# A chunked scan and a gated pair of matrix products on one core: a new order for the first scan, seven-product blocks for the second group, and an earlier place for each later group's y

## The chip, the core and the metric

The kernel runs on one NeuronCore of a Trainium2 chip. Five engines work side by side, each with its own instruction queue: TensorE (PE, matrix products into the accumulation memory PSUM), VectorE (DVE), ScalarE (ACT), GpSimd (POOL) and SyncE (SP), which here only issues transfers. Instructions on one queue start in the order in which they stand there; between queues, semaphores say when data is ready or a buffer is free.

The metric is the time of one execution on the device in microseconds (us). A profile records one further execution, instruction by instruction.

## The reference, cut to what matters

Two blocks follow each other. The first is a state-space scan over 4 x 8 heads, 768 positions, head size 32 and state size 16, in chunks. The second takes its output as 3072 tokens of 256 features and applies two matrix products with a gate between them. All is float32.

```python
# x, B, C: (4, 8, 768, 32|16|16);  a: (4, 8, 768), chunks of 32
la  = log(clip(a, 1e-6, 1));  cum = cumsum(la, within the chunk)
L   = exp(cum[i] - cum[j]) where i >= j, else 0
y   = ((C @ B.T) * L) @ x  +  (C @ state) * exp(cum)        # inside + carried in
state = exp(sum(la)) * state + (B * exp(cum[-1] - cum)).T @ x

x  = y as (3072, 256)
h  = x @ w_in                      # (3072, 2048)
g  = h * sigmoid(1.702 * h)
out = g @ w_out                    # (3072, 256)
```

## The kernel before, in words

**Tokens and groups.** The kernel works in chunks of 64 positions (two in a tile of 128), takes 256 positions as a *pair* (of tiles) and 512 tokens as a *group*: 12 pairs, 6 groups, two pairs to a group. Group 0 is pairs 0 and 1, group 1 is pairs 2 and 3, and so on. While the matrix products of group g run, the scan of the pairs of group g+1 and the loads of group g+2 are put between them. The order on each engine is the order in which the Python code issues the instructions (`in_order` ties each to the one before on its engine).

**One pair of the scan.** `differ` and `exps` (pairs 0 and 1) or `decay` (later pairs, a VectorE scan of 2.28 us) make the tile `L` of decay factors; `turn_only` transposes B and C on TensorE (`tp`, L514) and ScalarE or VectorE copies them out (L519, L521); `gain` (L591) multiplies B and x into the increments `A`, `keep` (L610, L622) adds them up to the states `S`; `score` (L560) multiplies C and B; `weigh` (L571) multiplies the scores into `L` on VectorE; `since_start` (L546) scales C; `finish` then makes y: `inter(0)` and `inter(1)` (L649) for what the states carry in, `intra` (L678) for what lies inside a chunk, in small matrix products on parts of the array, and two ScalarE copies (L702) to `yT`. A tiny GpSimd `memset` of `spare` (L666) stands between `inter(0)` and `inter(1)` as an order mark. Pair 1 is finished with `late=True`: `intra` first, then both `inter`.

**The weights** come as 64-bit numbers and are turned to float32 piece by piece, ten pieces in all: `fields` (L161, L164), `rounded` (L177) and `join` (L188, L194) on VectorE, `clamp` (L172, L173) on ScalarE. `narrow(i)` is rounded(i), fields(i+1), join(i).

**First product, plainly.** `hidden(g, f)` (L723) makes 128 hidden features for all 512 tokens with two products of 128 x 512; ScalarE applies the gate. `half` (L737) does it for 256 tokens of group 0, so that work can begin when only pair 0 is ready. Group 0 and group 1 use this form.

**First product, by seven.** For groups 2 to 5, `first(g, j, i)` treats a block of 256 features x 512 tokens as a 2 x 2 matrix of parts and uses seven products of 128 x 256 in place of eight. The steps `j.1 j.6 j.7 j.4` (L795) add up in one PSUM bank, `X`, and ScalarE copies the running sum out after each of the first three (L800: `ac`, `b`, `ac`), so each of them waits for the copy of the one before. The steps `j.5 j.2 j.3` (L805) add up in a second bank, `Y`. Then `j.D` (VectorE) adds `ac` to `Y`, a second addition (VectorE, inside `j.3`) adds `b`, and `j.S`, `j.T` and the end of `j.4` are ScalarE's gate. The sums of parts that this needs are `mix_in` of the weights (L757) and `mix_y` of `yT` (L763 to L765), on VectorE.

**Second product.** Group 0: `project_all` (L837). Groups 1 to 5: `product` (L896), again by seven, on sums `mix_w` of `w_out` (L862) and `mix_g` of the hidden block. A step `P` in the strings below is one of the seven products of one block: two of 128 x 128, four instructions in the records, since each float32 product is recorded as two.

**PSUM.** Products that don't add up over a whole group share four banks (`bank`, pool `ps`); a new tile waits until the readers of the tile that held its bank before are done.

**The order around the change.** The very first scan is written out call by call. Group 1 ran through a list of `H` (two `hidden`) and `P` (seven products of a block) with other work after each in `after`: the scan's `finish(later)` after `H3`. For later groups a string names the steps; the part that matters reads (block 2 and 3 of the first product, with `y` the scan of the next group and `w` its `weigh`):

```python
"2.1 1.S 1.4 1.3 2.6 2.5 2.2 2.7 1.T s 2.D 2.S w 2.4 3.1 2.3 3.5 2.T M0 3.6 "
"refill 3.7 y 3.2 3.D along 4.1 P P 3.4 P 3.S 4.6 P 3.3 4.5 3.T M1 P P 4.7 P 4.2 4.D M2"
```

Of the kernel before, what the change touches and what calls it, by code (L numbers as in the profile page):

```python
# [35 lines left out]
def kernel(  # L36
# [130 lines left out]
    def clamp(i):  # L167


        e = power[i]  # L170
        z = e.bitcast(FP32)
        nc.scalar.activation(z, e, AF.Relu, scale=-8.0, bias=edge[:, 0:1])  # L172
        nc.scalar.activation(e, z, AF.Relu, scale=-1.0, bias=edge[:, 1:2])  # L173
# [366 lines left out]
    def since_start(p, engine=nc.vector):  # L540

        b, c = divmod(2 * p, NC)
        s = st[p]
        tp = s.pop("tp")
        s["CsT"] = ssd.tile([P, 2, P], FP32, tag="CsT", name=f"CsT{p}", bufs=3)
        engine.tensor_tensor(out=s["CsT"], in0=tp, in1=since[b][:, c:c + 2], op=ALU.mult)  # L546
# [19 lines left out]
    def weigh(p, ks=(slice(0, 2),)):  # L566

        Lv = Ls[p].rearrange("p k r q i -> p k r (q i)")
        cb = st[p]["cb"].rearrange("p r k e -> p k r e")
        for k in ks:  # L570
            nc.vector.tensor_tensor(out=Lv[:, k], in0=Lv[:, k], in1=cb[:, k], op=ALU.mult)  # L571
# [51 lines left out]
                    out=new[:, m], in0=old, scalar=since[b][:, c + k, e:e + 1],  # L623
                    in1=new[:, m], op0=ALU.mult, op1=ALU.add)

    def finish(pairs, late=False):


        g, first = divmod(pairs[0], PG)
        y = [bank(f"y{pairs[0]}_{i}")[:, :NK * len(pairs) * 2 * H].rearrange(  # L630
            "p (t k i) -> p t k i", t=NK, i=H) for i in range(2)]
        begun, halves, seen = set(), {}, []

        def begin(i, parts):
            new = not begun & {(i, q) for q in parts}
            begun.update((i, q) for q in parts)
            return new

        def inter(flip):

            for n, p in enumerate(pairs):
                for k in range(2):
                    for i in range(2):
                        m, t = 2 * k + i, i ^ flip
                        if (4 * p + m) % (2 * NC) == 0:
                            continue
                        old = state[p][:, m - 1] if m else state[p - 1][:, 3]
                        rows = slice(HB * N * t, HB * N * (t + 1))
                        nc.tensor.matmul(  # L649
                            out=y[i][:, t, 2 * n + k], lhsT=old[rows],  # L650
                            rhs=st[p]["CsT"][rows, k, SIDES[i]],
                            start=begin(i, range(HB)), stop=False,
                            tile_position=(HB * N * t, 0), skip_group_check=True)
                        ins = tc.nc.cur_bb.bb.instructions[-1]
                        if not flip:
                            halves[i] = ins
                        elif seen:
                            tie(ins, seen.pop())

        def tie(ins, other):  # L660
            tc.add_manual_dep(ins, other.name, mybir.DependencyInfo(
                mybir.DependencyClass.Sync, mybir.DependencyReason.DATA), reason="same_bank")

        def part():

            nc.gpsimd.memset(spare, 0.0)  # L666
            ins = tc.nc.cur_bb.bb.instructions[-1]
            for other in halves.values():
                tie(ins, other)
            seen.append(ins)  # L670

        def intra(n, p):
            L = Ls[p]
            for k in range(2):
                for h in range(NH):
                    t, q = divmod(h, HB)
                    for i, side in enumerate(SIDES):
                        nc.tensor.matmul(  # L678
                            out=y[i][D * q:D * q + D, t, 2 * n + k], lhsT=rx[p][side, k, h],
                            rhs=L[side, k, h // Q, h % Q],  # L680
                            start=begin(i, (q,)), stop=True, tile_position=(H * i, D * q),
                            skip_group_check=True)

        if first == 0:
            yT[g] = ffn.tile([P, NK, TG], FP32, tag="yT", name=f"yT{g}")
        if not late:
            inter(0)
            part()
        for n, p in enumerate(pairs):
            intra(n, p)  # L690
        if late:
            inter(0)
            part()
        inter(1)
        for p in pairs:
            state.pop(p - 1, None)
            st.pop(p)
            Ls.pop(p)
        cols = slice(2 * first * P, 2 * (first + len(pairs)) * P)
        to = early_y if pairs[0] == 0 else yT[g][:, :, cols]  # L700
        for i in range(2):
            nc.scalar.activation(  # L702
                to.rearrange("p t (k s i) -> p s t k i", s=2, i=H)[:, i], y[i], AF.Copy)
        if pairs[0] == 0:
            nc.gpsimd.tensor_copy(yT[g][:, :, cols], to)
# [295 lines left out]
    ends(0, 0, nc.gpsimd)  # L1001
    ends(0, 1, nc.gpsimd)
    weigh(0)
    turn_only(1, ("ACT", "ACT", "ACT"))
    gain((0,))
    for r in range(2, R):
        ab[1, r] = bank(f"ab1_{r}")[:, :2 * Q * H]
# [1 line left out]
    differ(1, [(r, ab[1, r]) for r in range(2, R)])  # L1009
    exps(1, range(2, R))  # L1010
    since_start(0, nc.gpsimd)
    since_start(1, nc.gpsimd)
    keep(0)
    join(0)
    fields(1)
    score((1,))
    ends(1, 0)
    ends(1, 1)
    weigh(1, (0,))
    finish((0,))  # L1020
    clamp(1)
    table(AF.Silu)
    gain((1,))
    keep(1, (0, 1, 2))
    half(0, 0)
    weigh(1, (1,))
    finish((1,), late=True)
    rounded(1)
    join(1)
    load(PG)  # L1030
    spread_rows(1)
    fields(2)
    clamp(2)
    half(1, 0)
    keep(1, (3,))


# [31 lines left out]
       lambda: weigh(PG), lambda: weigh(PG + 1))  # L1069
    at(in_project[0], 9, lambda: narrow(9))  # L1070
    at(in_project[0], 11, lambda: finish(pairs))
    for i in range(4):
        at(in_project[0], 14, lambda i=i: mix_in(i))
    for k in range(PG):
        at(in_project[0], 8 + k, lambda k=k: load(2 * PG + k))
    for k, i in enumerate((9, 13)):
# [6 lines left out]
    at(after, "H0", lambda: decay(n), lambda: decay(n + 1), lambda: turn(n), lambda: turn(n + 1))  # L1083
    at(after, "H1", lambda: gain(later), lambda: score(later), lambda: keep(n),
       lambda: keep(n + 1), lambda: weigh(n), lambda: weigh(n + 1), lambda: spread(3 * PG))
    at(after, "H3", lambda: finish(later), lambda: load(p + 1), lambda: spread(3 * PG + 1))
    for k, i in enumerate(("H4", "P0", "P2", "P4")):
        at(after, i, lambda k=k: mix_w(k))
    for j in range(NF // 2):
        if j < 7:  # L1090
            at(after, f"P{min(j - 1, 4)}" if j else "H4", lambda j=j: mix_g(1, j))
    for k in range(PG):
        at(after, f"P{2 * k}", lambda k=k: decay(3 * PG + k))
    at(after, "P3", lambda: clip_rows(2), lambda: decay_rows(2))
    assert [b for b in range(NB) if 3 * CG <= b * NC < 4 * CG] == [2]


# [7 lines left out]
    project_all(0, in_project[0])  # L1105
    load(p)
    spread_rows(2)
    for step in "H0 H1 H2 H3 H4 P0 H5 P1 H6 P2 H7 P3 P4".split():
        j = int(step[1:])
        if step[0] == "H":  # L1110
            hidden(1, 2 * j)
            hidden(1, 2 * j + 1)
        else:
            product(1, j)
        for do in after.get(step, []):
            do()

    def run(g, steps, products=(), **do):
# [13 lines left out]
    def seven(g, j):  # L1132
        return [(g, j, (i,)) for i in ORDER]

    def ahead(g, p=None):

        pairs = (p, p + 1) if p else ()
        for k in pairs:
            turn_only(k)
        if pairs:  # L1140
            gain(pairs)
        for k in pairs:
            since_start(k)
        mix_y(g)
        for k in pairs:
            keep(k)

    run(1, "P P A P P P P P", seven(1, 5), A=lambda: ahead(2, p))
    mix_g(1, 7)

    for g in range(2, NG):
# [20 lines left out]

        if more:

            run(g, "2.1 1.S 1.4 1.3 2.6 2.5 2.2 2.7 1.T s 2.D 2.S w 2.4 3.1 2.3 3.5 2.T M0 3.6 "
                "refill 3.7 y 3.2 3.D along 4.1 P P 3.4 P 3.S 4.6 P 3.3 4.5 3.T M1 P P 4.7 P 4.2 4.D M2",
                seven(g, 0), s=lambda: score((n, n + 1)), w=lambda: (weigh(n), weigh(n + 1)),
                y=lambda: finish((n, n + 1)), refill=refill, along=along,
                M0=lambda: mix_g(g, 0), M1=lambda: mix_g(g, 1), M2=lambda: mix_g(g, 2))
            if most:  # L1180
                decay(p)
        else:
            run(g, "2.1 1.S 1.4 1.3 2.6 2.5 2.2 2.7 1.T 2.D M0 3.1 3.5 2.S 2.4 3.6 2.3 3.2 3.7 2.T 3.D M1",
                M0=lambda: mix_g(g, 0), M1=lambda: mix_g(g, 1))
        for j in range(5 if more else 4, NF // 2):
            h = "{1}.1 {0}.S P {0}.4 P {1}.6 P {0}.3 P {1}.7 {0}.T P {1}.5 P {1}.2 P {1}.D M".format(j - 1, j)
            run(g, h, seven(g, j - 4), M=lambda: mix_g(g, j - 2))
            if most and j == 6:
                decay(p + 1)
        k = NF // 2 - 1  # L1190
        run(g, f"P {k}.S P {k}.4 P P {k}.3 {k}.T P P P", seven(g, 4))
        if not more:
            for j in range(k - 1, k + 1):
                mix_g(g, j)
# [38 lines left out]
```

## Time and profile before

| | |
|---|---|
| time, median of 11 runs | 380.1 us (377.56 to 381.24) |
| profiled execution: its time, its span | 381.86 us, 380.1 us |
| TensorE busy | 369.0 us (97%), 3698 products |
| VectorE / ScalarE / GpSimd busy | 244.0 (64%) / 144.1 (38%) / 11.9 us (3%) |
| mean granted TensorE clock | 0.972 of full speed |
| transferred | 25.03 MB, mean 66 GB/s |

The span runs from the first to the last instruction; all times below are from its start. TensorE is busy nearly all the time, so the question in each stage is what the products there cost, how long it stands still, and at which clock it runs. The page draws the granted clock in 40 slices; a table of stretches gives it for any window. The end of a product in the records is modelled, so the distance from one start to the next is the better measure.

The stages, as the timeline of TensorE shows them: first scan to 31 us; group 0's first product to 56 us and second to 91 us; group 1 from 91 to 146 us (its blocks 2 to 7, with second products between, from 101 us); groups 2 to 5 from there, the scan of the next group at about 165, 226 and 284 us in groups 2, 3 and 4.

### The profile page before, as it was taken

The page shows a single profiled execution, that of the slowest core. Times are in us where ns is not written, and L with a number is a line of the kernel's source. Part 1 is how long each engine was busy: PE and PEld are TensorE (multiplying, and loading weights), DVE is VectorE, ACT ScalarE, POOL GpSimd, SP SyncE. Part 2 cuts the span into 40 slices and gives each one's busy share as a digit, 9 for nine tenths or more (in the row PEclk, how much of TensorE's full clock was granted, in tenths as well). Part 3 has the DMA queues.
Part 4 walks back from the last instruction along what each step waited for, and adds up shares of the span by engine and source line. Part 5 has one row for each costly group of instructions (what it writes and reads, how often), then busy time and mean ns, then how long its engine had stood idle before and what let it go on. Part 6 is the DMA issues. An engine that isn't in the chain of part 4 may idle for free.

```text
span 380.1 us, 8605 instructions
## 1 busy us (share of the span) xinstructions
PE 369.0 (97%) x3698; PEld 307.8 (81%) x3698; DVE 244.0 (64%) x457; ACT 144.1 (38%) x317; POOL 11.9 (3%) x42
## 2 busy tenths in 40 slices
PE   8799999999999999989999989999989999999996
PEld 4577448787567789879999969999968999989995
DVE  5877996996898617546776483766582436184453
ACT  5448836210432113533433353433353432363320
POOL 5210000000000000000000000000000000000000
PEclk9759999999999999988999999999999999999999
DMA  8888499025847100057100043000010000010001
GB/s 150 218 278 195 155 183 185 8 60 146 157 76 136 38 5 2 0 103 123 55 2 3 0 85 85 2 2 0 2 57 2 3 0 2 0 58 0 2 0 57
DMA packets 86029, 25.03 MB, mean 66 GB/s; under 512 B 76136, under 2 KB 79464, under 8 KB 85992
## 3 DMA queue, kind: packets, MB, share of 16 engines
q1 hardware_dynamic: 83544, 24.09, 28.6%
q10 hardware_dynamic: 2448, 0.39, 0.6%
q8 instruction: 29, 0.48, 0.5%
q14 instruction: 8, 0.07, 0.1%
HBM read 21.23 MB, written 3.24 MB: 64 GB/s over the span
## 4 chain that ended last, share of the span: by engine, by line
PE 82%; DVE 8%; DMA 4%; SPq 3%; ACT 1%; issue 1%; POOL 0%; DVEq 0%; POOLq 0%
PE acc L896 33%; PE X L795 13%; PE Y L805 10%; PE h L723 7%; PE o L837 5%; PE y L649 4%; PE y L678 3%; PE h L737 2%; DVE L L571 2%; PE cb L560 2%; SPq L123 1%; DMA b<-in_B_dram 1%; PE A L591 1%; DMA c<-in_C_dram 1%; PE tp L514 1%
## 5 line engine op out<-in xcount | busy, mean ns | idle before, releaser
L896 PEld LDWEIGHTS acc<-mw,mg 128*128 128x128 f32 x480 | 65.9, 191 | 3.5
L896 PE MATMUL acc<-mw,mg 128*128 128x128 f32 x480 | 67.6, 275 | 0.0
L914 DVE TENSOR_TENSOR gT<-Y,ac 128x512 f32<-128x512 f32 x32 | 22.1, 691 | 52.5 <-PE Y L805 50.6
L800 ACT ACTIVATE ac<-X 128x256 f32<-128x256 f32 x64 | 24.5, 383 | 74.9 <-PE X L795 74.4
L723 PE MATMUL h<-yT,w_in 128*128 128x512 f32 x112 | 49.9, 595 | 0.0
L896 PEld LDWEIGHTS acc<-w_out,gT 128*128 128x128 f32 x320 | 44.6, 195 | 4.2 <-issue 1.9
L896 PE MATMUL acc<-w_out,gT 128*128 128x128 f32 x320 | 45.5, 278 | 0.0
L772 ACT ACTIVATE gT<-gT 128x512 f32<-128x512 f32 x64 | 33.3, 520 | 27.3 <-DVE gT L914 26.9
L795 PE MATMUL X<-my,mi 128*128 128x256 f32 x128 | 38.6, 383 | 3.4 <-ACT b L800 3.4
L723 PEld LDWEIGHTS h<-yT,w_in 128*128 128x128 f32 x112 | 20.6, 190 | 23.0 <-issue 21.2
L914 DVE TENSOR_TENSOR gT<-Y,b 128x256 f32<-128x256 f32 x32 | 13.5, 422 | 31.1 <-PE Y L805 31.1
L726 ACT ACTIVATE gT<-h 128x512 f32<-128x512 f32 x28 | 16.6, 596 | 44.1 <-PE h L723 44.0
L763 DVE TENSOR_TENSOR mg<-gT 128x512 f32<-128x512 f32 x40 | 27.3, 683 | 8.7 <-PE acc L896 8.7
L837 PE MATMUL o<-w_out,gT 128*128 128x256 f32 x128 | 28.8, 381 | 0.0
L837 PEld LDWEIGHTS o<-w_out,gT 128*128 128x128 f32 x128 | 23.9, 190 | 3.4 <-issue 0.2
L795 PEld LDWEIGHTS X<-my,mi 128*128 128x128 f32 x128 | 20.1, 191 | 5.8 <-ACT b L800 4.6
L896 PE MATMUL acc<-mw,gT 128*128 128x128 f32 x160 | 24.3, 277 | 0.0
L896 PE MATMUL acc<-w_out,mg 128*128 128x128 f32 x160 | 24.0, 275 | 0.0
L896 PEld LDWEIGHTS acc<-mw,gT 128*128 128x128 f32 x160 | 22.7, 191 | 1.5
L896 PEld LDWEIGHTS acc<-w_out,mg 128*128 128x128 f32 x160 | 22.8, 191 | 1.2
L356 DVE TENSOR_TENSOR_SCAN L<-a,idents 128x1024 f32<-128x1024 f32 x9 | 20.5, 2283 | 0.0
L805 PE MATMUL Y<-yT,w_in 128*128 128x256 f32 x64 | 19.9, 394 | 0.0
(137 smaller groups left out, 521.8 us busy)
## 6 DMA issues: line engine op xcount, KB each, us to landing
a<-scratch SPq DMA_DIRECT2D x18, 256.0 KB
bits<-in_moe_w_out_dram SPq DMA_DIRECT2D x4, 1024.0 KB
x<-in_x_dram SPq DMA_DIRECT2D x24, 128.0 KB
out_dram<-c SPq DMA_DIRECT2D x9, 256.0 KB
bits<-in_moe_w_in_dram SPq DMA_DIRECT2D x4, 512.0 KB
bits<-in_moe_w_in_dram SPq DMA_DIRECT2D x2, 1024.0 KB
b<-in_B_dram SPq DMA_DIRECT2D x24, 64.0 KB
c<-in_C_dram SPq DMA_DIRECT2D x22, 64.0 KB
```

The costliest lines, as they stand in the source:

```text
L356: nc.vector.tensor_tensor_scan(out=L, data0=ra[p].rearrange("p k e -> p (k e)"), data1=idents.rearrange("p h i -> p (h i)"), initial=0.0, ...
L649: nc.tensor.matmul(out=y[i][:, t, 2 * n + k], lhsT=old[rows], rhs=st[p]["CsT"][rows, k, SIDES[i]], start=begin(i, range(HB)), stop=False, ...
L723: nc.tensor.matmul(out=h, lhsT=w_in[:, k, f * P:(f + 1) * P], rhs=yT[g][:, k], start=(k == 0), stop=(k == NK - 1))
L726: nc.scalar.activation(gT[g, j][:, i], h, AF.Silu, scale=GELU_SCALE)
L763: nc.vector.tensor_tensor(out=t[:, 0:2], in0=B[:, :, 1], in1=B[:, 0], op=ALU.subtract)
L772: nc.scalar.activation(o, i, AF.Silu, scale=GELU_SCALE)
L795: nc.tensor.matmul(out=s["X"], lhsT=lhsT, rhs=rhs, start=i == "1", stop=i == "4", skip_group_check=True)
L800: nc.scalar.activation(copy, s["X"], AF.Copy)
L805: nc.tensor.matmul(out=o, lhsT=lhsT, rhs=rhs, start=s.pop("new", False), stop=i != "5", skip_group_check=True)
L837: nc.tensor.matmul(out=o[k // 2][:, k % 2], lhsT=gT[g, f // 2][:, f % 2, k * P:(k + 1) * P], rhs=w_out[:, f], start=(f == 0 and k % 2 == 0 ...
L896: nc.tensor.matmul(out=acc[g][0][i][:, cols], lhsT=h[:, cols], rhs=w, start=(j == 0 and i in (0, 2, 5, 6) and k == 0), stop=(j == NF // 2 ...
L914: nc.vector.tensor_tensor(out=o, in0=v, in1=w, op=ALU.add)
```

## The change

**First scan.** Pair 1's transposes (`turn_only(1)`) move from before `gain((0,))` to behind the differences and exponentials of both pairs. Pair 1's `since_start` moves back; `ends(1, ...)` moves before `join(0)`, `gain((1,))` before `score((1,))`, `keep(1, ...)` is cut in other places, `weigh(1)` is done at once, and pair 1 is finished behind `half(1, 0)` in the ordinary order (`inter(0)`, `intra`, `inter(1)`): the argument `late` goes.

**Group 1.** Blocks 0 and 1 stay as they are; blocks 2 to 7 use the seven products. Blocks 2 and 3 run interleaved before the scan's y, block 4 with the second product of block 0, blocks 5 to 7 in the same pattern as later groups (now named `steady` and `closing`). `mix_y(1)` is new, `mix_in(0)` moves to the end of the group, and the loads and VectorE work that hung on `after` are spread anew.

**Later groups.** In block 3 the step `3.2` and `y` now stand between `3.6` and `3.7`; the loads (`refill`) follow y.

```diff
-    def finish(pairs, late=False):
+    def finish(pairs):
...
-        if not late:
-            inter(0)
-            part()
+        inter(0)
+
+        nc.gpsimd.memset(spare, 0.0)
+        seen.append(tc.nc.cur_bb.bb.instructions[-1])
+        for other in halves.values():
+            tie(seen[0], other)
         for n, p in enumerate(pairs):
             intra(n, p)
-        if late:
-            inter(0)
-            part()
         inter(1)
@@ first scan
     weigh(0)
-    turn_only(1, ("ACT", "ACT", "ACT"))
     gain((0,))
     for r in range(2, R):
         ab[1, r] = bank(f"ab1_{r}")[:, :2 * Q * H]
...
     exps(1, range(2, R))
     since_start(0, nc.gpsimd)
-    since_start(1, nc.gpsimd)
+    turn_only(1, ("ACT", "ACT", "ACT"))
     keep(0)
-    join(0)
-    fields(1)
-    score((1,))
     ends(1, 0)
     ends(1, 1)
-    weigh(1, (0,))
+    join(0)
     finish((0,))
+    fields(1)
+    gain((1,))
+    score((1,))
+    since_start(1, nc.gpsimd)
     clamp(1)
     table(AF.Silu)
-    gain((1,))
-    keep(1, (0, 1, 2))
     half(0, 0)
-    weigh(1, (1,))
-    finish((1,), late=True)
     rounded(1)
+    keep(1, (0,))
     join(1)
+    keep(1, (1, 2))
+    half(1, 0)
+    weigh(1)
     load(PG)
     spread_rows(1)
     fields(2)
+    finish((1,))
     clamp(2)
-    half(1, 0)
     keep(1, (3,))
@@ sums for group 1
-    for i in range(4):
-        at(in_project[0], 14, lambda i=i: mix_in(i))
+    at(in_project[0], 14, lambda: mix_in(1), lambda: mix_y(1), lambda: mix_in(2),
+       lambda: mix_in(3))
@@ group 1
-    for step in "H0 H1 H2 H3 H4 P0 H5 P1 H6 P2 H7 P3 P4".split():
...
+    for step in "H0", "H1":
+        for i in range(2):
+            hidden(1, 2 * int(step[1:]) + i)
+        for do in after[step]:
+            do()
...
+    def steady(j):
+        return "{1}.1 {0}.S P {0}.4 P {1}.6 P {0}.3 P {1}.7 {0}.T P {1}.5 P {1}.2 P {1}.D M".format(
+            j - 1, j)
+
+    def closing(k):
+        return f"P {k}.S P {k}.4 P P {k}.3 {k}.T P P P"
...
+    run(1, "2.1 3.1 2.5 2.6 3.6 2.2 2.7 3.5 3.7 3.2 2.D 2.4 3.D 3.4 2.S 3.S y L 2.3 2.T 3.3 3.T",
+        y=lambda: finish(later), L=more_loads)
+    mix_w(0)
+    for j in range(2):
+        mix_g(1, j)
+    run(1, "4.1 P P 4.6 P P 4.7 P 4.5 P 4.2 P 4.D", seven(1, 0))
+    mix_w(1)
+    mix_g(1, 2)
+    decay(p)
+    between = {5: (lambda: mix_g(1, 3), lambda: mix_w(2), lambda: clip_rows(2),
+                   lambda: decay_rows(2)),
+               6: (lambda: mix_g(1, 4), lambda: decay(p + 1)),
+               7: (lambda: mix_g(1, 5), lambda: mix_w(3))}
+    for j in range(5, NF // 2):
+        run(1, steady(j), seven(1, j - 4), M=lambda: [do() for do in between[j]])
+    k = NF // 2 - 1
+    run(1, closing(k), seven(1, 4))
+    mix_g(1, 6)
+    mix_in(0)
@@ later groups
-            run(g, "2.1 1.S 1.4 1.3 2.6 2.5 2.2 2.7 1.T s 2.D 2.S w 2.4 3.1 2.3 3.5 2.T M0 3.6 "
-                "refill 3.7 y 3.2 3.D along 4.1 P P 3.4 P 3.S 4.6 P 3.3 4.5 3.T M1 P P 4.7 P 4.2 4.D M2",
+            run(g, "2.1 1.S 1.4 1.3 2.6 2.5 2.2 2.7 1.T s 2.D 2.S w 2.4 3.1 2.3 3.5 2.T M0 3.6 3.2 y "
+                "refill 3.7 3.D along 4.1 P P 3.4 P 3.S 4.6 P 3.3 4.5 3.T M1 P P 4.7 P 4.2 4.D M2",
```

More of the change, by code (lines that the diff above doesn't have):

```diff
@@ L662, in tie @@
                 mybir.DependencyClass.Sync, mybir.DependencyReason.DATA), reason="same_bank")
[L664 to L670, printed above, removed]
         def intra(n, p):
@@ L1085 @@
        lambda: keep(n + 1), lambda: weigh(n), lambda: weigh(n + 1), lambda: spread(3 * PG))
[L1086 to L1094, printed above, removed]
     assert [b for b in range(NB) if 3 * CG <= b * NC < 4 * CG] == [2]
@@ L1107 @@
     spread_rows(2)
-    for step in "H0 H1 H2 H3 H4 P0 H5 P1 H6 P2 H7 P3 P4".split():
[L1109 to L1115, printed above, removed]
+    for step in "H0", "H1":
+        for i in range(2):
+            hidden(1, 2 * int(step[1:]) + i)
+        for do in after[step]:
             do()
@@ L1146, in ahead, with more_loads @@
             keep(k)
+    def more_loads():
+        load(p + 1)
+        spread(p + 1)
+    run(1, "2.1 3.1 2.5 2.6 3.6 2.2 2.7 3.5 3.7 3.2 2.D 2.4 3.D 3.4 2.S 3.S y L 2.3 2.T 3.3 3.T",
[17 more added lines that the diff above has]
+    mix_in(0)
     run(1, "P P A P P P P P", seven(1, 5), A=lambda: ahead(2, p))
@@ L1185 @@
         for j in range(5 if more else 4, NF // 2):
-            h = "{1}.1 {0}.S P {0}.4 P {1}.6 P {0}.3 P {1}.7 {0}.T P {1}.5 P {1}.2 P {1}.D M".format(j - 1, j)
-            run(g, h, seven(g, j - 4), M=lambda: mix_g(g, j - 2))
+            run(g, steady(j), seven(g, j - 4), M=lambda: mix_g(g, j - 2))
             if most and j == 6:
@@ L1190 @@
         k = NF // 2 - 1
-        run(g, f"P {k}.S P {k}.4 P P {k}.3 {k}.T P P P", seven(g, 4))
+        run(g, closing(k), seven(g, 4))
         if not more:
```

## The prediction

> **What bounds the kernel now.** I read the page's engine shares and clock row first, then the waits of TensorE alone, then the timeline at those waits, then tables of stretches for their clock.
>
> ```profile
> PE 369.0 (97%) x3698; PEld 307.8 (81%) x3698; DVE 244.0 (64%) x457; ACT 144.1 (38%) x317; POOL 11.9 (3%) x42
> ...
> PEclk9759999999999999988999999999999999999999
> ```
>
> TensorE is the bound, so a microsecond counts if it leaves TensorE's work, a standstill or half speed. The clock row has two dips, in slices of 9.5 us.
>
> ```profile
> PE X L795 <- ACT b L800: 3.4, 3, 1.1
> PE tp L514 <- DMA c<-in_C_dram: 1.5, 1, 1.5
> ```
>
> The waits (us in all, times, longest): block 3's X waits for ScalarE's copy `b` once in each of groups 2, 3, 4, and pair 1's transposes wait for C's transfer.
>
> ```profile
> 186.31 0.60 PE L795 MATMUL X<-my,w_in 128*128 128x256 f32 x2
> 186.74 0.61 PE L896 MATMUL acc<-w_out,gT 128*128 128x128 f32 x4
> 187.19 0.60 PE L795 MATMUL X<-my,mi 128*128 128x256 f32 x2
> ...
> 224.37 0.59 PE L795 MATMUL X<-my,mi 128*128 128x256 f32 x2
> ...
> 225.69 0.37 ACT L800 ACTIVATE b<-X 128x256 f32<-128x256 f32 x1
> 226.11 0.70 PE L795 MATMUL X<-my,mi 128*128 128x256 f32 x2 [1.15 <-ACT b L800]
> 226.74 1.11 PE L649 MATMUL y<-CsT,S 64*128 64x64 f32 x14
> ...
> 230.78 0.70 PE L795 MATMUL X<-yT,w_in 128*128 128x256 f32 x2
> ```
>
> In the timeline (start, length), a step of the seven takes 0.43 (186.31 to 186.74), a P 0.45 (186.74 to 187.19). At 224.37 step 3.6 starts; 3.7 must wait until 226.11, because ScalarE's queue held 2.T for VectorE's addition; y follows at 226.74, block 4's first product at 230.78.
>
> ```profile
> 14.00:15.00 1.00, 0.79 (x34) 0.31 (x18) 0.52 (x2) 1.00 (x4) 0.00 (x0) 0.50 1.14 197
> 27.00:28.00 1.00, 1.00 (x27) 0.73 (x10) 0.96 (x5) 0.00 (x0) 0.00 (x0) 0.70 1.00 80
> 164.15:167.56 3.41, 2.27 (x55) 1.64 (x54) 2.05 (x5) 1.07 (x3) 0.24 (x2) 1.00 0.55 55
> 167.56:174.38 6.82, 6.82 (x134) 6.17 (x122) 1.57 (x3) 1.47 (x3) 0.85 (x3) 0.50 0.68 131
> ```
>
> Columns: us, then busy time of TensorE, its loads, VectorE, ScalarE, GpSimd, then granted clock. It is 0.50 from about 14 to 27.6 and from 167.56 to 174.38: 4 and 2 steps of 3.41. Before each drop a window of that length held a standstill and small products: 1.55 idle before the first, 1.15 before the second (2.27 busy of 3.41). The stalls of groups 3 and 4 brought no drop.
>
> [...]products overlap in it (186.31 with length 0.60, the next at 186.74), so I price from start to start.
>
> **The change, part by part.**
>
> *y in groups 2 to 4.* No instruction is added; 3.2 and y go ahead of 3.7. Now: 3.6 at 224.37, stall, y, 4.1 at 230.78, so 6.41. After: 3.2 at 224.80. y's first matmul takes the bank of block 2's X, read last by 2.4's end on ScalarE at 223.65, so no wait; the second bank was block 2's Y, freed by the addition that ends at 225.33, so y starts at 225.4 and waits 0.15. y's length is 3.5 (226.74 to 230.23). 3.7 at 228.9 finds `b` (226.06) long done; 4.1 follows at 229.45, before held to 230.78 by y's eviction, which is earlier too. Gain 1.33, three times: −4.0. What is late next: 3.4 waits for the copy of 3.7, done at about 230.3 when P P reach it at 230.77; 3.3 waits for 3.D, ready 231.0, needed 232.5. Both hidden, by 0.5 and 1.5; without the two P the first would cost up to 0.4. `refill`'s DMAs (x and the next loads on SP) keep their order and wait for y's last read of x anyway; nothing of TensorE's is behind them.
>
> *Clock in group 2.* The 1.15 standstill in the window before 167.56 shrinks to about 0.15. If the drop goes with it: 3.6 to 4.1 takes 8.17 there (163.79 to 171.96) against 6.41 in group 3, so 1.76, and the 2.42 from 171.96 to 174.38 hold products of 1.21 at full clock: −3.0; bounds 0 (the drop stays) and −3.4 (half of 6.82).
>
> *First scan.* Pair 1's transposes move behind both pairs' differences, so C's wait of 1.54 is covered by 24 of those products. Step by step at full clock, with this trace's half-clock durations halved: the first differences end at 11.46; gain(0) 0.47; the masks wait for the exponentials, 12.6; differences 0.60 and 0.65, to 13.85; four transposes of 0.22, to 14.7 (c landed at 13.5); y of pair 0 waits for the third state addition on VectorE, 14.9; 0.72 inside and 0.45 carried, 16.25; gain(1) waits for ScalarE's copies of C, 17.05; scores, 17.75; half(0,0) 1.85, to 19.6; half(1,0) waits for join(1) on VectorE (its queue: Be 0.5, join(0) 1.37, fields 0.8, rounded 0.7, keep 0.6, join 1.4), to 20.65, ends 22.55; then keep and weigh (2 × 1.17) on VectorE, and y of pair 1 ends at 24.5, which ends at 28.9 before. Clamp(2) on ScalarE ends at 26.65 for 31.04. From 31.07 VectorE's chain of weight pieces sets group 0's pace almost without a gap, so what it gains stays: A (L591) starts at about 63.8.
>
> ```profile
> 68.33 0.78 PE L591 MATMUL A<-x,Be 64*32 64x64 f32 x54 [0.34 <-DVE CsT L546]
> ```
>
> So −4.4. Bounds: if the clock still halves at 14 until 27.6, half(1,0), now ahead of y of pair 1, costs 3.7 there, and A lands between −2 and +1.9.
>
> *Group 1.* A plain block before:
>
> ```profile
> 118.36 3.60 PE L723 MATMUL h<-yT,w_in 128*128 128x512 f32 x8
> 121.80 1.05 PE L896 MATMUL acc<-w_out,gT 128*128 128x128 f32 x8
> ```
>
> Blocks 2 to 7 lose this (3.44 a block) and get seven products, 7 × 0.43 = 3.01: 0.43 each, −2.6. Added on VectorE: six D and additions (0.69 + 0.42) and `mix_y` (1.5), 8.2; on ScalarE three copies (0.38) a block and gates in more pieces, some 1.4, so 8.4. VectorE is busy most of the time there:
>
> ```profile
> 101.00:111.70 10.70, 10.70 (x191) 6.22 (x176) 10.32 (x25) 2.39 (x4) 0.77 (x2) 1.00 0.48 81
> 124.90:131.40 6.50, 6.50 (x38) 4.59 (x37) 5.18 (x9) 1.20 (x2) 0.32 (x2) 1.00 0.04 8
> ```
>
> VectorE has 0.38 of room in the first stretch (columns as above) and 1.3 of 6.5 in the second, so not all hides. Walking its queue against TensorE's, the standstills are: 2.5 for gain's bank, freed by keep's first addition (102.57), 0.6; y for ScalarE's gates of 2.4 and 3.4, which read its banks, 0.55; block 4 0.6, where `mix_w(0)` and `mix_g` stand on VectorE behind 3.3's addition and P waits for them; 7.6 behind `clip_rows` and the scan of `decay_rows`, 0.15. Together 1.9, so −0.7; bounds −2.6 (all hide) and +2.5 (below). `mix_in(0)` (1.45), last in the group, is done 0.6 before its product; uncovered it would cost up to 1.45.
>
> *Sum*, against the profiled execution's own 381.86: −4.4 −0.7 −4.0 −3.0 = 369.8 (span 368.0). To the median, 380.1, that is −2.7%. The other executions of before run from 377.56[...].
>
> **Rivals.** *Half clock stays in the first scan (or in group 2).* For it: [...]small products still stand at 12 to 18 with waits of 0.65 and 0.3; against it: the wait of 1.54 is gone. The first scan then gives −2 to +1.9: 372.2 to 376.1, about 373.8; if only group 2's stays, 372.8. *Group 1 costs instead of saving.* VectorE's additions come late by what stands ahead of them (mix_g 1.5, decay 2.28, since-scan 1.76), ScalarE's copies are in order behind gates that wait for them, and X waits about 1 in five of the six blocks: −2.6 + 5.1 = +2.5 there, 373.0. For it: three such stalls in the later groups now; against it: groups 2 to 5 run the same pattern in blocks 5 to 7 without a wait in the list. *y's move gains nothing*, its second bank or 4.1 taking the stall over: 373.8. *Slower:* [...]the clock halves there and up to 34/2 = 17 are lost: 387. [...]the largest standstill of my walk there is 0.6, in block 4.
>
> **How the numbers follow.** As sketched, 369.8 (its own range 367.5 to 371.5): 0.55. Half clock in the first scan or group 2: 0.27. Group 1 costs: 0.11. y gains nothing: 0.03. Slower: 0.04. The range, 366.5 to 376, holds the sketch, group 1 with all its standstills hidden (367.9) and a little below, and the next three cases; it leaves out the last and the tails. About 0.3% (1.1 us) is what this kernel's measurement can tell from none. All cases but the last are below 379: faster 0.93, same 0.02 (rivals together), slower 0.05.
>
> **What would show it.** Right: clock 1.00 from 10 to 28 and 164 to 175; the transposes of pair 1 without C's wait; y of pair 1 done near 24.5 and A near 63.8; no `X <- ACT b` in block 3's row of waits; 4.1 starting 5.1 after 3.6; in group 1 blocks 5 to 7 of 7 × 0.435 + 7 × 0.445 = 6.2 where a hidden and a P block take 6.56. Wrong: a dip in the clock's row, A later than 66, a new wait of TensorE for ScalarE's copies or VectorE's additions in 100 to 146, or y waiting for its second bank by more than 0.5.

## The result, and the profile after

| | before | after |
|---|---|---|
| median | 379.21 us (47 runs, 373.5 to 381.62) | 371.74 us (12 runs, 369.86 to 373.68) |
| profiled execution: time, span | 381.86, 380.1 us | 373.68, 371.9 us |
| mean granted clock in it | 0.972 | 0.986 |

The ratio is 0.984 (0.9815 to 0.9862); the medians stand at 0.980. The ratio leaves out runs over 1.5% above the fastest of their kernel, which for before are most of those that lost the clock (ran at half of it) in more than one stretch. The forecast was 369.8, its range 366.5 to 376: 2.7% below the 380.1 measured then, where the medians fell by 2.0%.

The page of the changed kernel, engine shares and clock row:

```profile
PE 363.8 (98%) x3734; PEld 312.4 (84%) x3734; DVE 251.1 (68%) x472; ACT 150.8 (41%) x341; POOL 11.7 (3%) x42
...
PEclk9769999999999999999999999999999999999999
```

The dip of group 2 (slices 18 and 19) is gone; that of the first scan is still there. What TensorE waited for (us in all, times, longest; `issue` marks a standstill for which the records show no wait):

```profile
PE h L729 <- ACT yT L694: 0.7, 1, 0.7
PE y L649 <- issue: 0.5, 1, 0.5
PE Y L797 <- DVE S L610: 0.5, 1, 0.5
...
PE X L787 <- ACT ac L792: 0.2, 1, 0.2
```

The three stalls of block 3 and the wait for C have left the list. Among the new waits are these four of 0.2 to 0.7, three of them in group 1. The timeline of TensorE at block 3 of group 3 (start, length):

```profile
218.85 0.59 PE L787 MATMUL X<-my,mi 128*128 128x256 f32 x2
219.28 0.59 PE L797 MATMUL Y<-yT,w_in 128*128 128x256 f32 x2
219.81 1.16 PE L649 MATMUL y<-CsT,S 64*128 64x64 f32 x14
...
223.35 0.70 PE L787 MATMUL X<-my,mi 128*128 128x256 f32 x2
223.90 0.70 PE L787 MATMUL X<-yT,w_in 128*128 128x256 f32 x2
```

These are 3.6, 3.2, y, 3.7 and 4.1. From 3.6 to 4.1 it is 5.05, where it was 6.41; 3.7 finds its copy done.

The first scan, in a table of stretches (us, busy time of TensorE, its loads, VectorE, ScalarE, GpSimd, then granted clock), and where it ends to tell, at L591 of group 1's scan:

```profile
10.00:13.00 3.00, 2.70 (x98) 1.97 (x96) 2.97 (x5) 2.31 (x5) 1.20 (x2) 1.00 0.94 122
...
14.00:15.00 1.00, 1.00 (x8) 0.65 (x6) 0.93 (x4) 0.66 (x2) 0.00 (x0) 0.62 0.90 330
...
22.00:24.00 2.00, 2.00 (x6) 1.55 (x6) 1.97 (x5) 0.38 (x1) 0.00 (x0) 0.50 1.03 422
24.00:26.00 2.00, 2.00 (x12) 1.48 (x12) 1.96 (x7) 0.37 (x2) 0.00 (x0) 0.88 1.06 425
```
```profile
66.66 0.78 PE L591 MATMUL A<-x,Be 64*32 64x64 f32 x54 [0.34 <-DVE CsT L546]
```

Half clock from 14.24 to 24.48, 10.24 where before had 13.65 (13.96 to 27.61), though TensorE no longer stands still for C. And group 1, from its first plain product to group 2's first step, before and after:

```profile
91.42 3.60 PE L723 MATMUL h<-yT,w_in 128*128 128x512 f32 x8
...
108.21 1.11 PE L649 MATMUL y<-CsT,S 64*128 64x64 f32 x16
...
111.70 3.70 PE L723 MATMUL h<-yT,w_in 128*128 128x512 f32 x8
...
146.16 0.60 PE L795 MATMUL X<-yT,w_in 128*128 128x256 f32 x2
```

```profile
89.76 3.60 PE L715 MATMUL h<-yT,w_in 128*128 128x512 f32 x8
...
101.11 0.67 PE L797 MATMUL Y<-my,mi 128*128 128x256 f32 x2 [0.50 <-DVE S L610]
...
105.71 1.53 PE L649 MATMUL y<-CsT,S 64*128 64x64 f32 x16
107.17 1.48 PE L670 MATMUL y<-L,x 64*32 64x64 f32 x128
108.58 0.66 PE L649 MATMUL y<-CsT,S 64*128 64x64 f32 x7
109.78 0.67 PE L649 MATMUL y<-CsT,S 64*128 64x64 f32 x9 [0.54 <-issue]
110.38 1.13 PE L797 MATMUL Y<-yT,mi 128*128 128x256 f32 x4
...
145.11 0.60 PE L787 MATMUL X<-yT,w_in 128*128 128x256 f32 x2
```

y takes 4.67 here (105.71 to 110.38), where it took 3.49 (108.21 to 111.70) before.

So the span's 8.2 came from three places. Read from start to start in the two traces: up to group 1's first product −1.66 (91.42 to 89.76); group 1 up to group 2's first product +0.61 (54.74 to 55.35); groups 2 to 5, −7.15 (233.94 to 226.79), of which 3 × 1.36 is y's place and the rest, 3.07, the clock of group 2.

### The profile page after: what moved, and what is told of

Read it like the earlier page. It is cut to its first block, busy times and chain, and to the rows that moved or that the text cites. A ratio compares the mean times of both kernels' runs of the same rounds, so it can differ in the third digit from the quotient of the medians.

```text
span 371.9 us, 8716 instructions
## 1 busy us (share of the span) xinstructions
PE 363.8 (98%) x3734; PEld 312.4 (84%) x3734; DVE 251.1 (68%) x472; ACT 150.8 (41%) x341; POOL 11.7 (3%) x42
## 4 chain that ended last, share of the span: by engine, by line
PE 79%; DVE 8%; issue 7%; DMA 2%; ACT 1%; SPq 1%; POOL 0%; DVEq 0%; POOLq 0%
PE acc L888 31%; PE X L787 16%; PE Y L797 12%; PE o L829 5%; PE y L649 4%; PE y L670 2%; PE h L715 2%; PE h L729 2%; PE cb L560 2%; DMA b<-in_B_dram 1%; PE tp L514 1%; PE A L591 1%; DVE m L177 1%; PE busy L386 1%; DVE p L188 1%
## 5 line engine op out<-in xcount | busy, mean ns | idle before, releaser
L792 ACT ACTIVATE ac<-X 128x256 f32<-128x256 f32 x76 | 29.1, 382 | 81.1 <-PE X L787 80.6
L906 DVE TENSOR_TENSOR gT<-Y,ac 128x512 f32<-128x512 f32 x38 | 26.1, 690 | 48.8 <-PE Y L797 36.0
L764 ACT ACTIVATE gT<-gT 128x512 f32<-128x512 f32 (+1 forms) x76 | 39.4, 520 | 36.5 <-DVE gT L906 35.8
L787 PE MATMUL X<-my,mi 128*128 128x256 f32 x152 | 45.7, 383 | 0.2 <-ACT ac L792 0.2
L715 PE MATMUL h<-yT,w_in 128*128 128x512 f32 x64 | 28.5, 595 | 0.2 <-DVE w_in L194 0.2
L787 PEld LDWEIGHTS X<-my,mi 128*128 128x128 f32 x152 | 24.2, 191 | 1.7 <-ACT ac L792 0.3
L715 PEld LDWEIGHTS h<-yT,w_in 128*128 128x128 f32 x64 | 11.8, 190 | 14.1 <-issue 12.2
L797 PE MATMUL Y<-my,mi 128*128 128x256 f32 x76 | 22.8, 382 | 0.6 <-DVE S L610 0.5
L787 PE MATMUL X<-yT,w_in 128*128 128x256 f32 x76 | 22.9, 385 | 0.1
L787 PE MATMUL X<-my,w_in 128*128 128x256 f32 x76 | 22.8, 384 | 0.0
```

The source lines that it names most:

```text
L715: nc.tensor.matmul(out=h, lhsT=w_in[:, k, f * P:(f + 1) * P], rhs=yT[g][:, k], start=(k == 0), stop=(k == NK - 1))
L764: nc.scalar.activation(o, i, AF.Silu, scale=GELU_SCALE)
L787: nc.tensor.matmul(out=s["X"], lhsT=lhsT, rhs=rhs, start=i == "1", stop=i == "4", skip_group_check=True)
L792: nc.scalar.activation(copy, s["X"], AF.Copy)
L797: nc.tensor.matmul(out=o, lhsT=lhsT, rhs=rhs, start=s.pop("new", False), stop=i != "5", skip_group_check=True)
L906: nc.vector.tensor_tensor(out=o, in0=v, in1=w, op=ALU.add)
```

## The experiments

Every run reports its mean granted clock, so its time can be read beside it. In before's profile the clock is at half for 13.65 in the first scan and for 6.83 in group 2, and the mean is 0.972; in those of `y_only` and `y_filled`, with about 13.6 in the first scan and none in group 2, it is 0.980 and 0.982. No profile shows more than that in the first scan, so a mean of 0.977 or less is read here as a loss somewhere else as well. In the table, "full" means a mean of 0.997 or more; the runs of before are those made beside the experiments. Runs of one kernel at full clock still differ by up to 1.9 (`scan_y_filled`; the changed kernel by 1.4), so a single run is good to about 1.

| kernel | first scan | group 1 | y | runs | at full clock: runs, median us | the others: median us | all: median us |
|---|---|---|---|---|---|---|---|
| before | old | plain | old | 63 | 3, 374.0 | 379.7 | 379.5 |
| `scan_only` | new | plain | old | 22 | 9, 374.3 | 377.9 | 376.6 |
| `y_only` | old | plain | new | 6 | 1, 369.2 | 374.1 | 373.5 |
| `scan_y` | new | plain | new | 6 | 1, 370.0 | 373.5 | 373.3 |
| changed kernel (both sets) | new | seven | new | 18 | 11, 370.4 | 372.6 | 370.8 |
| `y_filled` | old | plain | old, stall filled | 21 | 2, 373.5 | 377.7 | 377.5 |
| `y_c_filled` | old, C's wait filled | plain | new | 6 | 3, 370.5 | 372.6 | 371.4 |
| `scan_y_filled` | new, two products more | plain | new | 6 | 6, 371.3 | none | 371.3 |
| `seven_reordered` | new | seven, new order | new | 6 | 4, 368.4 | 371.4 | 368.5 |
| `seven_fill1` | new, one product more | seven, new order | new | 6 | 6, 369.2 | none | 369.2 |
| `seven_fill2` | new, two products more | seven, new order | new | 6 | 6, 370.2 | none | 370.2 |

**One part at a time.** `y_only` is the kernel before with this edit:

```diff
-... M0 3.6 refill 3.7 y 3.2 3.D along ...
+... M0 3.6 3.2 y refill 3.7 3.D along ...
```

> Only the new place of y and 3.2 in groups 2, 3 and 4; first scan and group 1 as before. Theory (the forecast's): 3.7 no longer stalls, 3 x 1.35 = 4.0 us less where the clock of group 2 is full, and the half clock behind the stall of group 2 goes too, so 4.0 or 7.0 less: about 373.6 in all runs, apart from half clock in the first scan, ratio about 0.985. From 3.6 to 4.1 the trace shows 5.06. Rival (the half clock of group 2 comes from y's small products and not from the standstill): 4.0 less, with the dip of the clock still there in a part of the runs, ratio about 0.989.

Median 373.54, ratio 0.982 (0.977 to 0.987). Group 3 shows the gain at its place, 3.6 to 4.1 in 5.05:

```profile
219.32 0.60 PE L795 MATMUL X<-my,mi 128*128 128x256 f32 x2
...
224.37 0.70 PE L795 MATMUL X<-yT,w_in 128*128 128x256 f32 x2
```

Its stretch from 160 to 175 has a clock of 1.00, and no run's mean is below 0.98 (before: 35 of 63 at 0.977 or less). That goes with the theory. At full clock there is only one run, 369.2. The ratio is the whole change's (0.984) within the noise: most of what the change brings comes from this one edit.

`scan_only` is the other half: the functions and calls of the first scan as changed, all else as before.

> Only the first scan in its new order; groups 1 to 5 as before. If the standstill of 1.54 for C brings the half clock of the first scan: a clock of 1.00 from 10 to 28 in most runs and A (L591) near 63.8, 4.4 less. Rival, which the changed kernel's own profile speaks for: half clock comes all the same, since the products of 11 to 14 use only small parts of the array; then A near 66.7, 1.7 less, and as many runs with half clock as before. The dip of group 2 stays in either case in a part of the runs.

Neither prediction fits whole. 9 of 22 runs are at full clock (before 3 of 63), so the new order does make half clock rarer; but those 9 have a median of 374.3, and the three of before 374.0. At equal clock the new order gains nothing. In its profiled execution the first scan had some 3.2 at half clock (0.91 over 10 to 28; L591 at 65.43), and not at 14: the clock held there and fell near 21, behind a standstill that the new order itself makes, where half(1,0) waits for join(1) on VectorE.

```profile
PE h L729 <- DVE w_in L194: 2.2, 1, 2.2
```

So the new order has more than one place at which the clock fell, 14.24 in the changed kernel's profile and near 21 in this one. The profile has a second finding: group 2 was free of half clock (1.00 from 163 to 175) and group 4 had it (0.75 from 284 to 291), behind the same stall:

```profile
278.60 0.70 PE L787 MATMUL X<-my,mi 128*128 128x256 f32 x2 [1.14 <-ACT b L792]
279.23 1.11 PE L649 MATMUL y<-CsT,S 64*128 64x64 f32 x16
280.27 1.93 PE L670 MATMUL y<-L,x 64*32 64x64 f32 x128
282.13 1.97 PE L649 MATMUL y<-CsT,S 64*128 64x64 f32 x16
```

The first 16 instructions of y take 1.04, the last 16, at half clock, 1.9. So the drop came behind the stall of group 4 here and behind that of group 2 in before's profile, with stalls of 1.14 and 1.15.

`scan_y` leaves only group 1 out of the change.

> The whole change without its part on group 1: first scan and y new, group 1 with its plain blocks. The forecast's theory (seven products save 0.7 in group 1): 0.7 slower than the changed kernel, about 372.4. Rival, which the two profiles speak for (from group 1's first product to group 2's first one 54.74 before, 55.35 after): 0.6 faster than the changed kernel, about 371.1 on the median, 369.8 where the clock is full throughout.

Median 373.25, at full clock 370.0 (one run), where the changed kernel has 370.4 (11 runs). That difference is within the noise and does not tell the theory from the rival; the traces below find the two kernels level in group 1. The median is worse only by the share of full clock, one run of six, which says little with six runs. Its profiled execution was the one at full clock, and it shows the first scan as the forecast had laid it out:

```profile
19.97 1.97 PE L729 MATMUL h<-y,w_in 128*128 128x256 f32 x8 [1.03 <-DVE w_in L194]
...
62.80 0.78 PE L591 MATMUL A<-x,Be 64*32 64x64 f32 x54 [0.34 <-DVE CsT L546]
```

The wait of half(1,0) for join(1) is 1.03 (forecast 1.1), and L591 starts at 62.80; the first differences of this execution ended 0.6 earlier than the forecast's (10.90 for 11.46), so this is 63.4 for the forecast's 63.8. In group 1 it has a surprise, too: 55.31 from first product to first product (85.90 to 141.21), not before's 54.74, because a standstill that no wait explains lies in its y:

```profile
105.13 1.10 PE L649 MATMUL y<-CsT,S 64*128 64x64 f32 x15
106.62 0.21 PE L649 MATMUL y<-CsT,S 64*128 64x64 f32 x1 [0.38 <-issue]
```

The same stands in `scan_only` (0.44), in `scan_y_filled` (0.42) and in both profiles of the changed kernel (0.54 and 0.35), and in none of the four with the old first scan (before, `y_only`, `y_filled`, `y_c_filled`). So about 0.6 of group 1's +0.61 came with the new first scan, with plain blocks as with blocks by seven; against `scan_y` (55.31) the blocks by seven are level, 55.35 and 55.14 in the two profiles of the changed kernel.

**Is it the standstill that halves the clock?** `y_filled` keeps the old order and puts work into the stall of block 3. `fill_array` takes y's banks early and writes three products of ones there, which y overwrites:

```diff
-... M0 3.6 refill 3.7 y 3.2 ...
+... M0 3.6 fill refill 3.7 y 3.2 ...
+                fill=lambda: fill_array(n, 3),
+    def fill_array(p, n):
+        y_banks[p] = [bank(f"y{p}_{i}") for i in range(2)]
+        for i in range(n):
+            nc.tensor.matmul(out=y_banks[p][0][:, :2 * P], lhsT=ones, rhs=..., start=True, stop=True)
```

> The kernel before, with three more 128x256 products of ones (no result of theirs is used) between 3.6 and refill in groups 2, 3 and 4, in the bank that y starts in afterwards: they fill the standstill of 1.3 and leave the order of all else alone. Theory (the standstill in the window makes the clock halve in group 2): the dip of group 2 is gone in all runs, which takes 3.0 from those that had it; the stall's own time stays, 3.6 to 4.1 remains 6.4 everywhere; times near 377.6. Rival (the clock halves from y's small products, or from something else): the dip stays in as many runs as before and the times lie near 377.6 and 381 as before.

None of 21 runs has a mean clock at or below 0.977, where 35 of 63 of before have; the highest time is 378.58, before's 381.76. In group 2 of its profile, 3.6, the fill and 4.1, and the clock there:

```profile
162.69 0.59 PE L805 MATMUL X<-my,mi 128*128 128x256 f32 x2
163.12 1.46 PE L631 MATMUL y<-ones 128*128 128x256 f32 x6
...
169.09 0.70 PE L805 MATMUL X<-yT,w_in 128*128 128x256 f32 x2
```
```profile
163.00:180.00 17.00, 17.00 (x242) 15.16 (x241) 11.22 (x17) 6.58 (x16) 1.10 (x4) 1.00 0.59 90
```

3.6 to 4.1 still takes 6.40, and the clock is 1.00. Products that nobody uses, in a place where TensorE had to wait anyway, take some 2 off the median of all runs (377.5 for 379.5). In groups 2 to 4 the loss goes with the standstill: with it filled here (21 runs), or taken away without any added product in `y_only` (six runs), no run has a mean of 0.977 or less, though y's small products stand there as before.

`y_c_filled` does the same in the old first scan, on top of `y_only`: six small products of ones where the last transpose waits for C.

```diff
             for k in range(2):
+                if p == 1 and j == 1 and k == 1:
+                    for _ in range(6):
+                        nc.tensor.matmul(out=tp[:, j, k], lhsT=ones, rhs=ones, start=True, ...)
                 nc.tensor.transpose(out=tp[:, j, k], ...)
```

> The old first scan and plain group 1 with the new place of y (as y_only), and six 128x128 products of ones, used by nobody, in the place where pair 1's last transpose waits 1.5 for C (they write where that transpose writes afterwards): TensorE works through the standstill, and nothing is moved. Theory (the standstill is what makes the clock halve in the first scan): clock 1.00 from 10 to 28 in most runs, median about 369.5 (y_only at full clock 369.2). Rival (the small products of the differences do it): half clock in as many runs as y_only, median about 373.5.

Median 371.4, half way between the two, so neither fits whole. Three of six runs are at full clock, and the other three at 0.994, where `y_only` goes down to 0.98 and has one run of six at full clock. The profile says where the clock still falls:

```profile
20.35 0.30 PE L682 MATMUL y<-L,x 64*32 64x64 f32 x4
22.70 0.82 PE L682 MATMUL y<-L,x 64*32 64x64 f32 x60 [2.04 <-issue]
```
```profile
22.00:24.00 2.00, 1.30 (x68) 1.19 (x68) 1.93 (x7) 0.00 (x0) 0.00 (x0) 1.00 1.03 424
24.00:26.00 2.00, 1.72 (x13) 1.40 (x11) 1.33 (x4) 0.72 (x3) 0.34 (x2) 0.68 1.01 406
```

With C's wait filled the clock holds at 14 in this execution, and is at half for about 3.4, from 24.7 to 28.1, after the next long standstill, 2.04 inside y of pair 1, for which the trace names nothing that it waited for (VectorE's `weigh` was done at 20.9).

But the changed kernel's own dip at 14.3 has no long standstill before it: from 10 to 13 TensorE is idle 0.3 (2.70 busy of 3.00). What fills that stretch is small products, the differences. In `scan_y` and `seven_reordered` the same stretch is as busy (2.71 and 2.69 of 3.00), and there the clock held: such a stretch was followed by half clock in one execution and by full clock in two others. `scan_y_filled` adds two products over the whole array there (the rest of the bank of `ab1_1` takes them):

```diff
     gain((0,))
+    for _ in range(2):
+        nc.tensor.matmul(out=free, lhsT=ones, rhs=..., start=True, stop=True)
```

> The new first scan, plain group 1, y in its new place (as scan_y), and two 128x256 products of ones, used by nobody, behind gain of pair 0: 0.3 of their 0.86 falls into a standstill, 0.6 is added. Theory (full-array products in the window at 10 to 14 keep the clock up where the small ones alone don't): clock 1.00 in most runs, median about 370.5. Rival ([...]the small products of 14 to 18 bring the drop): half clock in as many runs as scan_y and the changed kernel (11 of 18), median about 373.

All six runs at full clock. The cost at full clock is 1.3 (371.3 for 370.0, one run), more than the 0.6 expected: the added products also waited, 0.57, for ScalarE's exponentials, whose bank they share.

```profile
12.14 1.13 PE L999 MATMUL ab<-ones 128*128 128x256 f32 x4 [0.57 <-ACT L L497]
```

With `seven_fill1` and `seven_fill2` below, the new order with such products had half clock in 0 of 18 runs, and without them (changed kernel, `scan_y`, `seven_reordered`) in 14 of 30. But 11 of these 14 are from earlier sets of runs; in the sets in which both kinds ran side by side it is 0 of 18 against 3 of 12, which can still be chance. The author's guess that little work of the whole array in the stretch before is what loses the clock, so that a standstill and small products both count, fits all of this and is not shown; nor is what makes the clock hold after the same stretch in one execution and fall in another.

**Where group 1 loses.** `seven_reordered` is the changed kernel with one string rewritten:

```diff
-2.1 3.1 2.5 2.6 3.6 2.2 2.7 3.5 3.7 3.2 2.D 2.4 3.D 3.4 2.S 3.S y L 2.3 2.T 3.3 3.T
+2.1 3.1 2.6 3.6 2.5 2.2 2.7 3.5 3.7 3.2 2.D 2.4 3.D 3.4 2.S 3.S 2.3 3.3 2.T 3.T y L
```

> The changed kernel with group 1's blocks 2 and 3 in another order: 2.6 and 3.6 ahead of 2.5, and y behind 2.3 and 3.3 instead of before them. Theory (group 1's 0.6 of loss is standstill: 0.8 at 2.5 for gain's bank, 1.2 within y for the gates that read its banks, 0.65 in block 4 for VectorE's mix_w and mix_g): about 1.5 of these 2.6 go, the stretch from group 1's first product to group 2's first is 53.9 instead of 55.35, times 1.5 below the changed kernel at the same clock. Rival (the time goes on something else, such as products that alternate between banks, or a new wait of 2.6 and 3.6 for their copies takes the place): 55 or more.

```profile
85.99 3.60 PE L715 MATMUL h<-yT,w_in 128*128 128x512 f32 x8
...
102.57 1.11 PE L649 MATMUL y<-CsT,S 64*128 64x64 f32 x16
103.61 1.48 PE L670 MATMUL y<-L,x 64*32 64x64 f32 x128
105.02 1.44 PE L649 MATMUL y<-CsT,S 64*128 64x64 f32 x16
106.39 0.70 PE L787 MATMUL X<-yT,w_in 128*128 128x256 f32 x2
...
139.86 0.60 PE L787 MATMUL X<-yT,w_in 128*128 128x256 f32 x2
```

Group 1 takes 53.87 (53.9 expected), y 3.82 where it took 4.67. At full clock the kernel runs at 368.4 for the changed kernel's 370.4, median 368.49, ratio to before 0.979 (0.973 to 0.985). Of the 1.48 that went, 0.60 lies before y, where gain's bank was, 0.58 in y together with 2.3 and 3.3, and 0.30 behind them, where VectorE's sums stand. But 0.4 of the 0.58 is the standstill without a wait, which is shorter here (0.33 for 0.75) for no reason that is known, so that 53.9 was met is in part luck, and what the gates alone cost is not shown. No product was added or taken away, so the loss was standstill, and the rival, that products which alternate between banks cost it, falls: they alternate as before. Against before's 54.74 the seven products now gain 0.87, about the 0.7 of the forecast.

**Both together.** One and two products of ones in the first scan of `seven_reordered`, and the changed kernel beside them:

> Group 1 reordered as in seven_reordered, and one 128x256 product of ones, used by nobody, behind gain of pair 0 in the first scan. Theory (full-array work in the window before 14 decides whether the clock halves): fewer runs with half clock than the third of seven_reordered, at 0.1 to 0.4 more at full clock: median about 368.8, no run above 370. Rival (one product is too little): as many runs at 371 to 372 as seven_reordered.

> The same with two such products. Theory: no run with half clock, as in scan_y_filled, at 0.6 to 0.9 more at full clock: about 369.2 in all runs. Rival: half clock in a third or more of the runs, up to 372.5.

> The changed kernel itself once more, beside the two others on one chip: 370.5 where the clock is full, 372.4 to 373.7 where it halves in the first scan, about half of the runs each. If the two kernels above are better only by their chip's share of full clock, this one comes down to 370.5 as well and stays 2 above seven_fill1; if the clock is what the products of ones change, it keeps its two groups of times.

369.19 (368.69 to 369.6), 370.17 (369.49 to 370.5) and 370.14 (369.66 to 371.81). With one product, too, all six runs are at full clock. It costs 0.8 there, more than the 0.1 to 0.4 expected, and the two cost 1.7. The changed kernel had five of six runs at full clock in this set and one at 0.995 with 371.81, not half of them; six runs tell that share badly. So this set does not show that the added product is what keeps the clock, and against the changed kernel beside it (369.8 at full clock) `seven_fill1` is 0.6 faster and `seven_fill2` 0.4 slower. The means of `seven_fill1` and `seven_reordered`, 369.2 and 369.4, are not told apart by so few; at best the added product buys even times rather than shorter ones.

## Why the prediction was right, and where not

**y in groups 2 to 4: right.** Forecast 1.33 each; measured 1.36 in groups 3 and 4 (6.41 to 5.05, and 6.61 to 5.25). Neither y's second bank nor a copy took the stall over.

**Clock in group 2: right in size and cause.** 3.0 forecast; 7.15 less 3 × 1.36 leaves 3.07. `y_filled` shows the cause with the order left alone: clock 1.00 in its group 2, and no mean of 0.977 or less in 21 runs. What the sum left out is that before has such a loss in only some of its runs (35 of 63), and that it need not fall in group 2: the sum put the whole 3.0 against one execution that had all of it, which is a reason why the median fell by less than that execution's span.

**First scan: the path right, the reading of the −4.4 wrong.** The steps hold: at full clock L591 stands at 62.80 in `scan_y`, 63.4 on the forecast's own start, and at 63.63 in the second profile of the changed kernel, for 63.8. The step that failed is "the wait of 1.54 is gone", taken as enough to keep the clock. In the profiled execution the clock halved all the same, and L591 moved by 1.67, inside the bounds given for that rival (−2 to +1.9). And the −4.4 compared a scan at full clock with one at half: at full clock both ways, the new order is worth nothing that these runs can tell (374.3 and 374.0, nine runs and three). What it brings, it brings by the clock: half clock in fewer runs (before 3 of 63 free of it, `scan_only` 9 of 22), for a shorter time (10.24 for 13.65 in the two profiles), and at a cost of 2.2 instead of about 4 (372.6 less 370.4 in the changed kernel; 377.7 less 373.5 in `y_filled`). The forecast did reckon the wait for join(1) (1.05), but not that the clock could fall behind this standstill, too, as in `scan_only` (0.91 over 10 to 28).

**Group 1: wrong sign in the trace, +0.61 for −0.7.** The saving was right: six plain blocks took 20.9 in before's trace, 42 steps at 0.433 are 18.2. The standstills were mis-sized, 3.4 in place of 1.9: 0.85 for 0.6 at 2.5 and the step behind it; 1.4 for 0.55 in y; 0.65 for 0.6 in block 4; 0.4 for 0.15 at 7.6; 0.1 after y. Of y's 1.4, 0.6 is the gates' wait, as foreseen; the rest, 0.75 (0.56 in the second profile), is the standstill without a wait, which costs 0.6 with plain blocks as well and was in no step of the forecast. So the steps that failed are two: the walk of the queues gave the listed standstills 0.7 too little, and one of them it could not see.

**The sum.** 371.74 lies between the two likeliest cases, 369.8 and 373.8, because the kernel does both: 370.4 at full clock in 11 of 18 runs, 372.6 in the others. The parts add up at full clock: before's 374.0, less 4.1 for y, more 0.6 for group 1, nothing for the first scan, is 370.5. The forecast, without its two terms of the clock in before, started from about 374.5 and took off 4.0 and 0.7. That 369.8 lies within 0.6 of 370.4 is therefore in part luck: group 1 came out 1.3 worse, the start 0.5 better. The slower rival, half clock in group 1 from 111 to 145, whose 387 was an estimate by the length of that stretch, did not come: in both profiles of the changed kernel the clock of group 1 is 1.00.

Read at full clock, then, only y's place makes the kernel faster: `y_only` has 369.2 there, the whole change 370.4. As far as one run of `y_only` can tell, the other two parts cost about 1 at that clock, 0.6 of it the standstill that came with the new first scan, and the new first scan gives more back by its share of full clock (all runs: 370.8 for 373.5, six runs of `y_only`).

## What to carry to other kernels

A short standstill next to many small products can cost more by the clock than by its length: in group 2 of before the stall was 1.15 and the half clock behind it cost 3.07. Look at the stretch before a drop, and ask how long TensorE stands still in it and between what. Fill it with work that has to be done anyway, and if there is none, products that nobody uses may pay, where TensorE waits in any case (377.5 for 379.5 in `y_filled`). Where one string sets the order of several engines, count what each step finds in its bank: two moves in it took 1.5 off group 1 in the traces (1.4 to 2.0 in the times at full clock), where the new form of the blocks had brought nothing. And compare kernels at the same clock before saying what a part is worth.

## What was not expected of the hardware

Half clock for 13.65 followed a standstill of 1.54 in the old scan, and half clock for 10.24 followed a stretch with 0.3 of standstill and small products in the new (2.70 busy of 3.00), which in two other executions (2.71 and 2.69) held the clock. The same program has the loss in some executions and not in others (before is at full clock in 3 of 63 runs), and it came behind one or another of three equal stalls (group 2 in before, group 4 in `scan_only`). A standstill of 1.15 beside small products stood ahead of the loss in group 2 of before, and stalls of the same length in groups 3 and 4 brought none there; with 1.3 of products of ones in their place none of 21 runs has a mean of 0.977 or less.

The standstill of 0.35 to 0.54 in y of group 1 stays open. It has a fixed place in the order of instructions: in `scan_y` it stands behind the 15th record of y's last part, and in `scan_y_filled`, which has two products (four records) more in the first scan, behind the 11th. In the changed kernel it stands behind the 7th record of that part; `seven_fill2` has eight records more ahead of it (2.3 and 3.3, and two products of ones), and there a standstill lies behind the 127th of the 128 records of the part before, eight records earlier.

```profile
106.38 0.88 PE L649 MATMUL y<-CsT,S 64*128 64x64 f32 x11
107.68 0.44 PE L649 MATMUL y<-CsT,S 64*128 64x64 f32 x5 [0.42 <-issue]
```
```profile
105.08 1.47 PE L670 MATMUL y<-L,x 64*32 64x64 f32 x127
106.85 0.21 PE L670 MATMUL y<-L,x 64*32 64x64 f32 x1 [0.31 <-issue]
```

The first two lines are `scan_y_filled`, the other two `seven_fill2`. So the standstill moves with the number of records ahead of it and does not stay with one product. What TensorE waits for there was not shown, nor why the four profiles with the old first scan are free of it.
